# A prefetch hint at the head of the program for the branch over a fallback path

## The chip, the cores and the metric

The kernel runs on one core of one Trainium2 chip. The metric is the device time of one execution in microseconds; three runs of the kernel before took 587.13, 588.6 and 590.96 us, and their median, 588.6 us, is its time. Engines are named as in the profile: PE (TensorE, with PEld for its weight loads), DVE (VectorE), ACT (ScalarE), POOL (GpSimd) and SP (SyncE, which issues the transfers). Each engine has a sequencer that reads its own program, and each program has its own copy of every branch.

## What is computed

A linear attention with a decay per row of the state, and behind it a gated feed-forward layer. B is 4, H 8, S 768, D 48; there are 3072 tokens, 384 features and 1536 hidden features.

```python
state = np.zeros((B, H, D, D))
for t in range(S):
    state = alpha[:, :, t, :, None] * state + np.einsum('bhd,bhe->bhde', k[:, :, t], v[:, :, t])
    y[:, :, t] = np.einsum('bhd,bhde->bhe', q[:, :, t], state)
x = y.transpose(0, 2, 1, 3).reshape(B * S, H * D)
g = x @ w_gate
out = (g / (1 + np.exp(-g)) * (x @ w_val)) @ w_out
```

q, k, v and alpha are 32-bit floats; the three weight matrices arrive as 64-bit floats.

## The kernel before, in words

`tile_kernel` (L1053 to L1065) calls `main_path`, which does all of the work for inputs in the expected ranges, and behind it a branch to `general_path`, a slow second version for any input.

`main_path` cuts the sequence into 16 units of 192 steps, each of three chunks of 64, and computes the recurrence with products on PE (scores, carry, outputs) and scans on DVE. The rows are packed into blocks of 384 tokens. For each of the 8 blocks there are 12 steps over the hidden features: the gate and value products (L692), the silu on ACT (L700), the product with the value on DVE (L704), and the output product (L724). Every factor is split into a high and a low part, and three of the four part products are taken. Weights are cut from 64 bits to single precision by three operations on raw words (L148, L151, L154). The order of everything is written out by hand in the table `ORDER`, one word per step with a letter for the engine (t PE, v DVE, s ACT, g POOL, y SP), and played back at L889 to L896 without a scheduler moving anything.

In parallel the kernel checks that alpha and the weights lie in the ranges for which this method is exact enough. Each check leaves 1 or 0 per partition; a product with ones (L911) sums them, and L912 writes the sum into `flag`: 128 when all partitions are in range. Then come

```python
        ok = nc.values_load(flag[0:1, 0:1], min_val=0, max_val=P)
        with tc.If(ok < P):
            general_path(tc, *args, scratch)
```

at L1063 to L1065. In each engine's program this is a TENSOR_LOAD of the flag into a register (L1063) and a compare-and-branch (L1064). For the inputs timed here the flag is 128, so every engine branches over its part of the general path, which lies directly behind the compare, to a short tail: waits on the semaphores of what this engine, or on SP its transfers, had in flight (also L1064), then, on SP, waits on all of them once more, and twice a barrier of all engines with a clearing of semaphores between (L1091, the line that opens and closes the tile context). SP's last work ahead of the branch is the store of the last three tiles of the result (L741, tiles `ot`), which wait for ACT's copies out of PSUM (L736).

How far the jump goes differs by engine. In rows of the program (one row can stand for several equal instructions), the compare stands at row 1905 of 2457 on PE, 503 of 2281 on DVE, 475 of 681 on ACT, 121 of 138 on POOL and 397 of 615 on SP; the tail is at the end of each.

## Time and profile before

| what | value |
|---|---|
| median of three runs (lowest, highest) | 588.6 us (587.13, 590.96) |
| span of the profiled execution | 586.7 us |
| PE busy | 560.2 us, 95% |
| DVE, ACT, POOL busy | 405.7, 258.9, 128.0 us |
| mean granted TensorE clock | 0.990 |
| last matmul ends | 577.75 us |
| last data packet of a store ends | 581.27 us |

The span runs from the first to the last instruction of the program on any engine; the profile gives no device time of that same execution beside it, so the runs stand above it. Register, branch, semaphore and transfer-issuing instructions are not counted as busy; they show in the view of one source line, under the engine's name with a q (SPq is SP's sequencer, PEldq that of PE). There a row gives the operation, how often it occurs, its shortest, median and longest time in ns, and the start of the first and of the last in us. The view of transfers names the queues that fetch code "instruction".

### The profile page before, as it was taken

The numbers are of one execution on the slowest core, as the hardware profiler recorded it, in microseconds if no ns is written. First come the engines' busy times: TensorE is split into PE (matmuls) and PEld (weight loads), VectorE is DVE, ScalarE is ACT, GpSimd is POOL, SyncE is SP. The second block draws the span as 40 slices with busy tenths as digits, with TensorE's granted clock in tenths as the row PEclk, the third lists the DMA queues.
The fourth block names the chain that finished last, engine by engine and source line by source line (L and its number), as shares of the span: only waits on it lengthen the run. The fifth ranks groups of instructions, "written<-read, shape, count | busy, mean of one in ns | idle before, by whom it ended". The sixth has DMA issues, their size and how long they took to land.

```text
span 586.7 us, 13794 instructions
## 1 busy us (share of the span) xinstructions
PE 560.2 (95%) x5555; PEld 531.0 (91%) x5555; DVE 405.7 (69%) x625; ACT 258.9 (44%) x599; POOL 128.0 (22%) x122
## 2 busy tenths in 40 slices
PE   9899897998999999999999999999999999999993
PEld 4677786888999999999999999999999999999993
DVE  7789999998898999939989859885942321121120
ACT  5587542342331222232326664646565656542121
POOL 6115443452323221222120101400001110001110
PEclk9989999998999999999999999999999999999998
DMA  7799945322235853336485858774553362200001
GB/s 238 243 290 247 332 111 117 82 63 66 76 98 127 199 161 91 85 75 145 105 203 141 192 155 227 198 193 153 175 126 104 92 171 63 62 27 15 1 0 47
DMA packets 95368, 77.67 MB, mean 132 GB/s; under 512 B 32832, under 2 KB 92224, under 8 KB 95296
## 3 DMA queue, kind: packets, MB, share of 16 engines
q1 hardware_dynamic: 95296, 76.71, 49.1%
q8 instruction: 45, 0.74, 0.5%
q14 instruction: 27, 0.22, 0.1%
HBM read 62.52 MB, written 5.90 MB: 117 GB/s over the span
## 4 chain that ended last, share of the span: by engine, by line
PE 77%; DVE 10%; DMA 7%; issue 2%; SPq 2%; POOL 0%; ACT 0%; DVEq 0%
PE v L692 23%; PE ops L724 23%; PE g L692 22%; DMA raw<-in_moe_w_val_dram 3%; PE early_ps L766 2%; PE A L553 2%; DMA raw<-in_moe_w_out_dram 2%; PE s L530 2%; PE y L619 2%; DVE t L151 2%; DVE t L154 1%; DMA raw<-in_moe_w_gate_dram 1%; DVE h L704 1%; DMA L<-in_k_dram 1%; DVE t L148 1%
## 5 line engine op out<-in xcount | busy, mean ns | idle before, releaser
L692 PE MATMUL v<-xT,w 128*128 128x384 f32 x864 | 168.7, 339 | 8.4 <-DVE h L704 8.4
L692 PE MATMUL g<-xT,w 128*128 128x384 f32 x864 | 167.8, 338 | 0.1
L692 PEld LDWEIGHTS v<-xT,w 128*128 128x128 f32 x864 | 151.3, 189 | 11.1 <-DVE h L704 10.3
L724 PE MATMUL ops<-w,hh 128*128 128x384 f32 x576 | 157.7, 337 | 0.0
L692 PEld LDWEIGHTS g<-xT,w 128*128 128x128 f32 x864 | 151.6, 188 | 1.8 <-ACT h L700 0.6
L713 POOL TENSOR_TENSOR hl<-h,hh 128x384 fp32r<-128x384 f32 x54 | 57.6, 1067 | 304.5 <-ACT hh L708 293.5
L704 DVE TENSOR_TENSOR h<-h,v 128x384 f32<-128x384 f32 x96 | 52.9, 551 | 102.5 <-PE v L692 101.1
L708 ACT CAST hh<-h 128x384 fp32r<-128x384 f32 x96 | 49.2, 513 | 140.5 <-DVE h L704 73.8
L724 PEld LDWEIGHTS ops<-w,hh 128*128 128x128 f32 x576 | 105.2, 188 | 0.8
L724 PE MATMUL ops<-w,hl 128*128 128x384 f32 x288 | 97.0, 337 | 1.6 <-DVE hl L713 1.5
L700 ACT ACTIVATE h<-g 128x384 f32<-128x384 f32 x96 | 47.0, 489 | 104.3 <-PE g L692 92.0
L505 DVE STREAM_TRANSPOSE K<-Gs 32x384 f32<-32x384 f32 x96 | 54.7, 570 | 2.4 <-PE A L553 0.6
L724 PEld LDWEIGHTS ops<-w,hl 128*128 128x128 f32 x288 | 54.1, 188 | 2.5 <-DVE hl L713 2.1
L713 DVE TENSOR_TENSOR hl<-h,hh 128x384 fp32r<-128x384 f32 x42 | 26.4, 628 | 26.0 <-ACT hh L708 25.5
L325 POOL TENSOR_TENSOR w<-t,w 128x768 fp32r<-128x768 f32 (+1 forms) x17 | 36.4, 2152 | 30.2 <-ACT w L321 21.3
L448 DVE TENSOR_TENSOR_SCAN AT<-AT,back 128x771 f32<-128x771 f32 x16 | 33.8, 2115 | 0.6
L563 DVE TENSOR_TENSOR X<-s,mask 64x384 f32<-64x384 f32 (+1 forms) x48 | 26.0, 553 | 10.1 <-PE s L530 8.0
L464 POOL TENSOR_TENSOR X<-trq,AT 112x768 f32<-112x768 f32 x9 | 15.8, 1759 | 57.4 <-DMA xT<-X 23.6
L439 DVE TENSOR_TENSOR_SCAN Gs<-AT,inj 128x772 f32<-128x772 f32 x16 | 28.2, 1761 | 0.2
L321 ACT CAST w<-t 128x768 fp32r<-128x768 f32 (+1 forms) x20 | 15.4, 774 | 23.0 <-DVE t L154 22.9
L297 ACT ACTIVATE wc<-wc,wbias 128x384 f32<-128x384 f32 x36 | 23.4, 649 | 1.2
L154 DVE SCALAR_TENSOR_TENSOR t<-raw,t 128x768 uint32<-128x768 uint32 (+1 forms) x20 | 21.4, 1070 | 0.5
(112 smaller groups left out, 591.0 us busy)
## 6 DMA issues: line engine op xcount, KB each, us to landing
xT<-X SPq DMA_DIRECT2D x84, 72.0 KB, 2.2
raw<-in_moe_w_gate_dram SPq DMA_DIRECT2D x12, 384.0 KB, 7.2
raw<-in_moe_w_val_dram SPq DMA_DIRECT2D x12, 384.0 KB, 7.8
V<-in_v_dram SPq DMA_DIRECT2D x96, 48.0 KB, 3.0
raw<-in_moe_w_out_dram SPq DMA_DIRECT2D x12, 384.0 KB, 8.2
wc<-in_moe_w_gate_dram SPq DMA_DIRECT2D x12, 384.0 KB, 5.1
wc<-in_moe_w_val_dram SPq DMA_DIRECT2D x12, 384.0 KB, 3.7
wc<-in_moe_w_out_dram SPq DMA_DIRECT2D x12, 384.0 KB, 4.6
```

Of the source, the lines that this page charges most:

```text
L154: lambda: nc.vector.scalar_tensor_tensor(out=t, in0=lo, scalar=29, in1=t, op0=ALU.logical_shift_right, op1=ALU.bitwise_or),
L325: eng.tensor_tensor(out=lo, in0=src, in1=hi.bitcast(F32), op=ALU.subtract)
L439: nc.vector.tensor_tensor_scan(*(x.rearrange("p g t -> p (g t)")[:, ::-1] for x in (Gs, AT, inj)), 0.0, op0=ALU.mult, op1=ALU.add)
L448: nc.vector.tensor_tensor_scan(Af, Af, back[:, 1 : n + 1], back[:, 0:1], op0=ALU.mult, op1=ALU.add)
L505: nc.vector.transpose(out=bass.AP(k0.tensor, k0.offset, [k0.ap[0], (G * 2 * D, NU), (2 * D, G), (1, 32)]), in_=Kg[j * BO + x : j * BO + x ...
L563: nc.vector.tensor_tensor(out=X[r, z, f * GF : (f + 1) * GF, :].rearrange("r g (c t) -> r g c t", c=NU), in0=sps[f][r].rearrange("r g (c t ...
L692: nc.tensor.matmul(pt, wsp[kind, f][a][:, kt * P : (kt + 1) * P], xT[blk][:, b_, kt, :], start=(n == 0), stop=(n == 3 * KT - 1),)
L700: nc.scalar.activation(h, acc.pop(("g", blk, f)), AF.Silu)
L704: nc.vector.tensor_tensor(out=h, in0=h, in1=acc.pop(("v", blk, f)), op=ALU.mult)
L708: nc.scalar.copy(out=hh, in_=acc["h", blk, f])
L713: eng.tensor_tensor(out=hl, in0=acc.pop(("h", blk, f)), in1=hh.bitcast(F32), op=ALU.subtract)
L724: nc.tensor.matmul(ops[blk][i], h[b_][:, i * P : (i + 1) * P], wsp["o", f][a], start=(first and n == 0), stop=(last and n == 2),)
```

## The change

In front of the playback of `ORDER` one call is added, and the branch is given a label that the call names:

```diff
@@ main_path
             todo[f"wc{i}"] = lambda eng, i=i: range_check(i)
+    tc.mark_branch_hint_location(
+        "right", "LikelyTaken", engines=[e.engine for e in (nc.sync, nc.scalar, nc.vector, nc.tensor, nc.gpsimd)]
+    )
     BANKS = ("A0", "A1", "A2", "ops0", "ops1", "vps", "gps")
@@ tile_kernel
-        with tc.If(ok < P):
+        with tc.If(ok < P, label="right"):
             general_path(tc, *args, scratch)
```

In the built program this is one instruction on each of the five engines, BRANCH_PREFETCH_HINT, which names the branch with that label on the same engine and says that it is likely taken. Although the call stands behind the allocation and clearing of the tiles in the source, the instruction comes out in front of them, second in each program behind the jump that enters the tile context. Nothing else differs in kind, order or waits on any engine; line numbers grow by three (L1064 is L1067 in the changed kernel, L1091 is L1094) and the numbers in the names of tiles by five. SP's program before begins

```order
L1091 UNCONDITIONAL_BRANCH
L423 DMA Le<-in_alpha_dram 128x2x288
L280 DMA raw_132<-in_moe_w_gate_dram 128x3x256
L280 DMA raw_134<-in_moe_w_val_dram 128x3x256
L423 DMA Le<-in_q_dram 128x2x288
```

and with the change

```order
L1094 UNCONDITIONAL_BRANCH
L1094 BRANCH_PREFETCH_HINT
L423 DMA Le<-in_alpha_dram 128x2x288
L280 DMA raw_137<-in_moe_w_gate_dram 128x3x256
L280 DMA raw_139<-in_moe_w_val_dram 128x3x256
L423 DMA Le<-in_q_dram 128x2x288
```

where `Le` and `raw` are tiles for alpha and for raw weights: the hint stands ahead of the first transfer. Around the branch SP's rows with the change are

```order
L1066 TENSOR_LOAD flag
L1066 ISA x2
L741 DMA out_dram<-ot_0_11_6435 128x384
L741 DMA out_dram<-ot_1_11_6437 128x384
L741 DMA out_dram<-ot_2_11_6478 128x384
L741 DMA out_dram<-ot_0_11_6830 128x384
L741 DMA out_dram<-ot_1_11_6832 128x384
L741 DMA out_dram<-ot_2_11_6835 128x384
L1067 COMPARE_AND_BRANCH
L946 COMPARE_AND_BRANCH
L946 UNCONDITIONAL_BRANCH x2
L1094 BRANCH_PREFETCH_HINT
```

The compare at L1067 is the branch that the hint names; the rows behind it belong to the general path, whose two loops had hints of their own for their back edges before the change too. These rows are the same in the kernel before, but for the numbers.

## The prediction

> **What bounds the kernel now.** I read the page first (engines, slices, queues, chain), then the chain in order of time, then everything that stands behind the last matmul, because the change touches one branch and that branch stands there. From the page:

> ```profile
> span 586.7 us, 13794 instructions
> PE 560.2 (95%) x5555; PEld 531.0 (91%) x5555; DVE 405.7 (69%) x625; ACT 258.9 (44%) x599; POOL 128.0 (22%) x122
> PE   9899897998999999999999999999999999999993
> ...
> q8 instruction: 45, 0.74, 0.5%
> q14 instruction: 27, 0.22, 0.1%
> ```

> TensorE (PE) is busy 95% of the span and in every slice but the last. The last two rows are code: the instructions themselves come by DMA, in 45 packets of 16 KB (0.74 MB over 45) on one queue and some 27 of 8 KB on the other. PE has 5555 matmuls and as many weight loads, 11,110 instructions; over 45 packets that is 247 each, so the 16 KB queue feeds PE (about 64 bytes an instruction, 256 to a block), and the 8 KB blocks of the other four engines hold 128. The last slice has PE at 3 tenths. The chain in order of time ends so:

> ```profile
> 571.50 6.26 PE ops L724 x36
> 577.76 0.02 issue
> 577.78 0.48 ACT ot L736
> ```

> and the window view, cut at the last matmul, at the last store's issue and at the end of its data, is

> ```profile
> 577.75:579.60 1.85, 0.00 (x0) 0.00 (x0) 0.00 (x0) 0.48 (x1) 0.00 (x0) 1.00 0.45 153
> 579.60:581.27 1.67, 0.00 (x0) 0.00 (x0) 0.00 (x0) 0.00 (x0) 0.00 (x0) 1.00 0.60 208
> 581.27:586.67 5.40, 0.00 (x0) 0.00 (x0) 0.00 (x0) 0.00 (x0) 0.00 (x0) 0.57 0.02 6
> ```

> (columns: length, then busy time of PE, its loads, DVE, ACT, POOL, the clock, DMA share, GB/s). So 8.9 us lie behind the last matmul, and in the last 5.4 us no engine computes and almost no data moves. What those hold, the view of the branch's line shows; a q behind an engine's name is its sequencer, and the last columns are first and last start:

> ```profile
> L1064 SPq EVENT_SEMAPHORE  x8: 17/17/17, 583.3 to 583.9; - x8
> L1064 POOLq COMPARE_BRANCH  x1: 45/45/45, 567.1 to 567.1; - x1
> L1064 POOLq EVENT_SEMAPHORE  x1: 17/17/17, 567.6 to 567.6; - x1
> L1064 DVEq COMPARE_BRANCH  x1: 72/72/72, 575.8 to 575.8; - x1
> L1064 PEldq COMPARE_BRANCH  x1: 3502/3502/3502, 576.4 to 576.4; - x1
> L1064 ACTq COMPARE_BRANCH  x1: 50/50/50, 578.6 to 578.6; - x1
> L1064 DVEq EVENT_SEMAPHORE  x1: 21/21/21, 578.7 to 578.7; - x1
> L1064 SPq COMPARE_BRANCH  x1: 50/50/50, 579.7 to 579.7; - x1
> L1064 PEldq EVENT_SEMAPHORE  x1: 51/51/51, 580.0 to 580.0; - x1
> L1064 ACTq EVENT_SEMAPHORE  x1: 17/17/17, 581.3 to 581.3; - x1
> ```

> From its branch to its next instruction POOL takes 0.5 us (567.1 to 567.6), DVE 2.9, ACT 2.7, PE 3.6, SP 3.6. POOL has 15 rows of program between its compare and the end, so its jump stays within a block of where it is; the others jump over hundreds. What SP does in that time is nothing: the waits of its queue have

> ```profile
> SPq L1064 <- SPq L1064: 3.7, 1, 3.7
> ```

> a wait on itself. I read these gaps as the fetch of the block that holds the jump's target. [...]

> SP is the last, and behind its eight waits comes a second hole, in the rows of the closing barrier's line, asked for in two windows:

> ```profile
> L1091 SPq EVENT_SEMAPHORE  x2: 28/28/28, 584.0 to 584.1; - x2
> ...
> L1091 SPq EVENT_SEMAPHORE  x8: 17/28/28, 585.5 to 586.6; - x8
> ```

> Two go at 584.0 and 584.1, the next at 585.5: 1.4 us. The code queue in the window 583.5 to 585 has

> ```profile
> q14 instruction: 1, 0.01, 2.1%
> ```

> one 8 KB block. So the jump's target lies near the end of its block, and the next one is asked for only after SP has arrived there. SP's arrival sets the end. ACT, the latest of the other four, stands in the barrier at 581.4:

> ```profile
> L1091 ACTq DRAIN  x2: 8/8/8, 581.4 to 586.2; - x2
> ```

> **The change part by part.** It adds one instruction per engine behind the entry jump, and takes nothing away. I take two terms.

> *The hint's own time.* No hint has run in this trace. The nearest rows are sequencer instructions of the same kind, SP's register moves in the entry (L1080) and the branches above (45 to 72 ns):

> ```profile
> L1080 SPq MOVE  x4: 29/34/42, 0.0 to 0.2; - x4
> ```

> Five engines execute it side by side, so once 0.03 to 0.07 us counts; it is on the path, since the chain starts with them. Above it is bounded by 3.7, if an engine stood still until the block asked for had come; below by nothing, as it removes no work. I take 0.1, by the moves, because a prefetch that stalls its engine would be none.

> *The end.* If the target's block is there when SP branches, SP goes on after 0.5 us as POOL did, at 579.7 + 0.5 = 580.2. It then meets its waits for the stores. The last three stores' rows:

> ```profile
> L741 SPq DMA_DIRECT2D out_dram<-ot x3: 332/332/1095, 577.2 to 579.3; - x3
> ...
> DMA to landing us min/median/max: 2.5/2.6/3.5
> ```

> The last was issued at 579.3 and landed 2.5 later, at 581.8. What was hidden in the fetch till now, the landing, is late next. The eight waits took 0.6 us in a row (583.3 to 583.9); about half of them come behind the landing, 582.1, and the two of the closing line make it 582.3. The following block was ready 2.2 us after SP's arrival in the target's block (583.3 to 585.5); counted from 580.2 that is 582.4, nearly the same instant. From there the end is as before, 586.7 - 585.5 = 1.2 us, so 583.6: a gain of 3.1 us. Bounds: at most 3.3, if the following block is there too (the landing then decides: 582.3 - 0.1 + 1.2 = 583.4); at least nothing, if the target's block isn't there. The added instruction moves every block's end by one instruction, which at 0.08 us each is inside the rounding.

> [...]

> DVE, PE and ACT would save 2.2 to 3.1 us each at their branch, which is worth nothing: they wait in the barrier for SP. The general path is not run, so its loops' own hints play no part.

> Sum: -3.1 + 0.1 = -3.0 us on a span of 586.7, so 583.7. The page has no time of that execution beside its span; the runs have a median of 588.6, 1.9 above the span, and I keep that difference: **585.6 us**.

> **The rivals.**

> *Lost on the way, 588.7 us.* The hint is the first instruction, the branch comes 570 us later; PE refills 45 times in between. If the block is fetched at once, the refills push it out before it is needed, and all that is left is the hint's 0.1. For this: the place, and that all refills seen are in sequence. Against: the hint names a branch by its label, and an instruction that names the branch can be kept until that branch's own block comes in; SP also passes few blocks, its 8 KB packets being a share of 27. [...]

> *The wrong side, 588.7 us.* The condition written, flag below 128, is the one for the general path. If "taken" means that side, the hint asks for the block right behind the branch, which comes in sequence anyway. For this: the text of the change. Against: the general path stands right behind the branch, so the machine's taken jump is the skip, and the four long gaps are paid on that jump.

> *The hint displaces a refill, slower.* While the hint is armed, its block takes the place of the block that comes next in sequence, and an engine waits at the block's end as SP does at 584.1. Place: PE's refills; price: 1.4 us each. One costs less than the end gives (588.7 - 3.1 + 1.4 = 587.0 us); from the third on it decides (589.8), and if all 45 are hit it is 588.7 - 3.1 + 63 = 648.6 us. For it: a prefetcher that has to hold one more block. Against: a refill has 586.7/45 = 13 us of room, and its packets take 0.5% of the DMA engines.

> *A stall in front, 592.3 us.* The hint waits for its fetch (3.7) and the block is lost later: 588.6 + 3.7. Against it: this puts two of the doubtful things together.

> **How the numbers follow.** The forecast has 0.65: the fetch is plainly in the rows and SP stands idle for it, and the doubt is the distance. Lost on the way 0.17, the wrong side 0.07, a refill displaced 0.07 (0.04 of it in the many-refill form), a stall in front 0.04. The forecast's own range is 585.6 with its term's bound (0.2 lower) and the spread of the runs shown (587.1 to 591.0, so -1.5 and +2.4): 583.9 to 588.0. The two cases of no effect, 0.24 together, need 588.7 inside with some spread above it; I leave out the stall and the many refills, and end at 589.3. The runs before lie 0.65% apart, so 1%, 5.9 us, is about what a measurement tells from no change: the forecast, -0.5%, and both cases of no effect lie inside. Faster by over 1% would take the full gain and a median nearly 3 us low, 0.03; slower by over 1% is the many refills and a little of the stall, 0.05; within 1%, 0.92.

> **What would show it.** Right: SP's first wait of the branch's line 0.5 us after its branch instead of 3.6, with the same for DVE, ACT and PE; SP's closing waits reached by 582.4 and no hole over 0.3 us; the code packets for the target's blocks earlier than the branch; the hint's row at the front under 0.1 us. Lost on the way or the wrong side: SP's gap again 3.6 and the code packet behind the branch; for the first, extra code packets in the first microseconds; for the second, none. A displaced refill: holes between PE's matmuls at block ends, which the chain calls issue. I'd be wrong altogether if SP were held by the barrier instead: another engine arriving after SP.

## The result, and the profile after

| | before | with the hint |
|---|---|---|
| median (lowest, highest) of 10 runs | 588.98 us (585.01, 591.78) | 585.7 us (582.64, 587.46) |
| span of the profiled execution | 586.7 us | 584.0 us |
| last matmul ends | 577.75 | 577.88 |
| SP's branch starts | 579.7 | 580.1 |
| from SP's branch to the end | 7.0 | 3.9 |

The ratio of the times is 0.9945, with a 95% interval of 0.992 to 0.997: 0.55% faster, 3.2 us. In the two profiles all of it lies behind SP's branch. The rows of the branch's line in the changed kernel (L1067):

```profile
L1067 SPq EVENT_SEMAPHORE  x8: 17/17/17, 582.0 to 582.6; - x8
L1067 POOLq COMPARE_BRANCH  x1: 59/59/59, 567.2 to 567.2; - x1
L1067 POOLq EVENT_SEMAPHORE  x1: 17/17/17, 567.7 to 567.7; - x1
L1067 DVEq COMPARE_BRANCH  x1: 84/84/84, 576.0 to 576.0; - x1
L1067 PEldq COMPARE_BRANCH  x1: 398/398/398, 576.6 to 576.6; - x1
L1067 DVEq EVENT_SEMAPHORE  x1: 21/21/21, 576.6 to 576.6; - x1
...
L1067 ACTq COMPARE_BRANCH  x1: 68/68/68, 578.7 to 578.7; - x1
L1067 ACTq EVENT_SEMAPHORE  x1: 17/17/17, 579.2 to 579.2; - x1
L1067 SPq COMPARE_BRANCH  x1: 70/70/70, 580.1 to 580.1; - x1
```

DVE goes on 0.6 us after its branch (2.9 before), ACT 0.5 (2.7), and PE's branch takes 398 ns instead of 3502. SP goes on after 2.0 us (1.97 before the starts are rounded to 580.1 and 582.0), 1.7 less than before, yet about four times as long as DVE and ACT. The line that closes the tile context (L1094):

```profile
L1094 SPq EVENT_SEMAPHORE  x10: 17/28/28, 582.6 to 583.9; - x10
...
L1094 POOLq BRANCH_PREFETCH_HINT  x1: 51/51/51, 0.8 to 0.8; - x1
L1094 SPq BRANCH_PREFETCH_HINT  x1: 65/65/65, 0.8 to 0.8; - x1
L1094 ACTq BRANCH_PREFETCH_HINT  x1: 45/45/45, 0.8 to 0.8; - x1
L1094 DVEq BRANCH_PREFETCH_HINT  x1: 51/51/51, 0.9 to 0.9; - x1
L1094 PEldq BRANCH_PREFETCH_HINT  x1: 50/50/50, 0.9 to 0.9; - x1
```

SP's ten closing waits take 1.3 us (582.6 to 583.9) where they took 2.6 (584.0 to 586.6): the hole of 1.4 us behind the second of them is gone. The hints cost 45 to 65 ns each. The windows, cut as before at the last matmul, in the last store and at the end of its data:

```profile
577.88:580.00 2.12, 0.00 (x1) 0.00 (x0) 0.00 (x0) 0.48 (x1) 0.00 (x0) 1.00 0.40 139
580.00:581.65 1.65, 0.00 (x0) 0.00 (x0) 0.00 (x0) 0.00 (x0) 0.00 (x0) 1.00 0.52 189
581.65:583.97 2.32, 0.00 (x0) 0.00 (x0) 0.00 (x0) 0.00 (x0) 0.00 (x0) 0.79 0.01 4
```

The idle stretch behind the data has gone from 5.4 to 2.3 us; the stretch ahead of it has grown a little. So the 3.1 us from branch to end are two pieces, 1.7 of SP's gap and 1.4 of the hole; 0.4 is given back ahead of the branch. There the last matmul ends 0.1 us later than before, and the longest of SP's last three stores takes 1325 ns to issue instead of 1095:

```profile
L741 SPq DMA_DIRECT2D out_dram<-ot x3: 332/333/1325, 577.4 to 579.7; - x3
...
DMA to landing us min/median/max: 2.3/2.8/3.6
```

### The profile page after: what moved, and what is told of

It reads as the page before. It is cut to its first block, busy times and chain, and to the rows that moved or that the text cites. A ratio compares the mean times of both kernels' runs of the same rounds, so it can differ in the third digit from the quotient of the medians.

```text
span 584.0 us, 13799 instructions
## 1 busy us (share of the span) xinstructions
PE 561.9 (96%) x5555; PEld 532.6 (91%) x5555; DVE 406.0 (70%) x625; ACT 258.8 (44%) x599; POOL 126.9 (22%) x122
## 4 chain that ended last, share of the span: by engine, by line
PE 77%; DVE 11%; DMA 6%; issue 2%; SPq 2%; POOL 0%; ACT 0%; DVEq 0%
PE ops L724 23%; PE v L692 23%; PE g L692 22%; DMA raw<-in_moe_w_gate_dram 2%; DVE t L151 2%; PE early_ps L766 2%; PE A L553 2%; PE s L530 2%; PE y L619 2%; DMA raw<-in_moe_w_out_dram 2%; DMA raw<-in_moe_w_val_dram 1%; DVE t L154 1%; DMA L<-in_k_dram 1%; DVE h L704 1%; DVE t L148 1%
## 5 line engine op out<-in xcount | busy, mean ns | idle before, releaser
L724 PE MATMUL ops<-w,hh 128*128 128x384 f32 x576 | 157.7, 337 | 0.0
L724 PEld LDWEIGHTS ops<-w,hh 128*128 128x128 f32 x576 | 105.2, 188 | 0.8
L724 PE MATMUL ops<-w,hl 128*128 128x384 f32 x288 | 97.0, 337 | 1.5 <-DVE hl L713 1.5
L724 PEld LDWEIGHTS ops<-w,hl 128*128 128x128 f32 x288 | 54.1, 188 | 2.4 <-DVE hl L713 2.1
L553 PE MATMUL A<-V,K 64*48 64x48 f32 (+1 forms) x720 | 21.5, 207 | 0.5 <-DVE X L563 0.3
```

The costliest lines, as they stand in the source:

```text
L553: nc.tensor.matmul(to[j * BO : j * BO + D, g - gs.start, :], Ks[r, x, g, KC[j]], Vd[r, x, g, VC[j]], start=(x == 0 or not whole), stop=(x ...
L724: nc.tensor.matmul(ops[blk][i], h[b_][:, i * P : (i + 1) * P], wsp["o", f][a], start=(first and n == 0), stop=(last and n == 2),)
```

## The experiments

Theory A, formed on these rows: the hint makes an engine fetch the jump's target on entering the code block that holds the branch, instead of the block next in sequence, and SP enters that block only half a microsecond ahead of its branch, which is why it still waits; only SP's jump counts. The rivals stand in each expectation. The profiled executions differ by a few microseconds in the body ahead, so the traces are compared from SP's branch to the end, and the times by their ratio to the kernel before on the same chip. Gaps are differences of printed starts, so they can be off by 0.1 us.

| run | SP's gap behind its branch, us | hole in the closing waits | branch to end | ratio to before (95%) |
|---|---|---|---|---|
| before | 3.6 | 1.4 | 7.0 | 1 |
| the change | 2.0 | none | 3.9 | 0.9945 (0.992 to 0.997) |
| hint on SP alone | 1.9 | none | 3.9 | 0.9949 (0.9926 to 0.9971) |
| hint on all but SP | 3.4 | none | 5.4 | 0.9976 (0.9947 to 1.0006) |
| one drain, no hint | 3.3 | 1.6 | 6.9 | 1.0005 (0.9974 to 1.0036) |
| twelve drains, no hint | 2.9 | none | 4.8 | 0.9943 (0.992 to 0.9966) |
| hint, eleven drains | 0.5 | none | 3.6 | 0.9922 (0.9898 to 0.9947) |
| hint, one drain | 0.7 | none | 4.0 | 0.9958 (0.9939 to 0.9977) |
| hint, eleven drains, drain on PE | 0.5 | none | 3.3 | 0.9929 (0.99 to 0.9959) |
| drain on PE, no hint | 3.4 | 1.5 | 6.8 | 0.999 (0.9967 to 1.0013) |
| no branch | - | - | - | 0.9926 (0.9893 to 0.9959) |

The intervals of the runs with the hint on SP, of twelve drains and of no branch all lie below 1 and overlap, so the times don't rank these runs. What is said below of single pieces rests on the traces, one execution each.

Two things in the traces bear on theory A. First, the start of the block that holds the branch shows as a pause of about 0.35 us in front of one of SP's instructions: its last store in the kernel before, the instruction ahead of that store with the change or with one drain, the middle store with the hint and one drain. In the kernel before, SP has such a pause, of 0.34 to 0.36 us, at 160.71, 244.91, 325.68, 398.50 and 579.27 us, each time 128 of its rows after the last; so the prediction's 128 to a block holds for SP, and PE's 16 KB packets start 255 of PE's rows apart in the mean of 42 intervals. By this the branch's block starts 0.4, 0.5 and 1.7 us ahead of the branch. Second, in the seven traces with such a pause an 8 KB code packet starts 0.7 to 0.8 us behind the block's start. Their queue is not SP's alone (in the kernel before, packets on it start at 576.86, 1.0 us behind DVE's branch, and at 579.30, 0.7 behind ACT's); I take as SP's the packets that no branch or arrival of another engine explains.

**The hint on SP alone.**

```diff
-    tc.mark_branch_hint_location(
-        "right", "LikelyTaken", engines=[e.engine for e in (nc.sync, nc.scalar, nc.vector, nc.tensor, nc.gpsimd)]
-    )
+    tc.mark_branch_hint_location("right", "LikelyTaken", engines=[e.engine for e in (nc.sync,)])
```

> The hint on SP alone. Theory A (the armed hint makes SP, on entering the block that holds the branch, fetch the jump's target in place of the block next in sequence; only SP's jump sets the end): all of the gain is here. SP goes on 2.0 us after its branch, no hole in the closing waits, span 2.7 us under the 586.7 of before, time about 585.8; the gaps of DVE, PE and ACT are back at 2.9, 3.6 and 2.7 us. Rival B (an engine other than SP also counts): part of the gain is missing, 587 or more. Rival C (the added instruction only moved SP's code to other places in its blocks) gives the same as A here.

Measured: 585.38 us. The rows of its branch's line:

```profile
L1065 SPq EVENT_SEMAPHORE  x8: 17/17/17, 582.5 to 583.1; - x8
...
L1065 PEldq COMPARE_BRANCH  x1: 3842/3842/3842, 576.9 to 576.9; - x1
...
L1065 SPq COMPARE_BRANCH  x1: 70/70/70, 580.6 to 580.6; - x1
```

The whole gain is there with PE (3842 ns), DVE and ACT paying for their jumps as before. Rival B falls: what the other four save is worth nothing.

**The hint on all but SP.**

```diff
-    tc.mark_branch_hint_location(
-        "right", "LikelyTaken", engines=[e.engine for e in (nc.sync, nc.scalar, nc.vector, nc.tensor, nc.gpsimd)]
-    )
+    tc.mark_branch_hint_location("right", "LikelyTaken", engines=[e.engine for e in (nc.scalar, nc.vector, nc.tensor, nc.gpsimd)])
```

> The hint on the other four engines. Theory A and rival C: no gain, time as before (588.6 to 589), SP's gap 3.7 and the hole of 1.4 us in its closing waits as before, although DVE, PE and ACT go on 0.5 to 0.6 us after their branches. Rival B: part of the gain, 1 us or more.

Measured: 586.27 us; the interval of its ratio holds 1, so a gain shows in the trace alone. SP's rows in the branch's line and in the closing one (here L1092):

```profile
L1065 SPq EVENT_SEMAPHORE  x8: 17/17/17, 581.4 to 582.0; - x8
...
L1065 SPq COMPARE_BRANCH  x1: 50/50/50, 578.0 to 578.0; - x1
```
```profile
L1092 SPq EVENT_SEMAPHORE  x10: 17/28/28, 582.0 to 583.3; - x10
```

I expected no gain, and theory A missed half of what happened. The gap is nearly as long as before, 3.4 us, but the hole is gone (ten waits in 1.3 us), although SP's instructions are those of the kernel before. The built program shows one difference on SP: the label that the skip jumps to carries a mark on all engines, be the hint on all five, on these four or on SP alone, and none without a hint. I conclude that the marked target is put at the start of a code block, so that SP needs no second one. The trace agrees: a next block starts to come at 582.2, 0.8 us behind SP's arrival, and SP runs to its end without waiting for it, where in the kernel before the next block starts 0.6 us behind SP's arrival and SP stands for it. That the mark is what moves the target is argued from these rows and the next run, not seen by itself. So the hole goes with hints on the other four engines alone, and only the 1.7 us of the gap need the hint on SP.

**One drain on SP instead of the hint.**

```diff
         for word in ORDER.split():
+            if word == "y:Lc0":
+                for _ in range(1):
+                    nc.sync.drain(fusable=False)
```

> No hint; one drain more in SP's program at a place where SP has time, so that everything behind it stands one instruction later, as with the hint. Rival C: the gain is as with the hint, SP's gap 2.0, no hole, span about 584. Theory A: SP's gap stays over 3 us (its fetch of the block next in sequence starts one instruction earlier, so 3.2 to 3.7), the gain is under 0.6 us; the hole of 1.4 us may stay or go, and tells whether it hangs on the hint or on the place of the target in its block: if it goes, 2 us of gain in all at most.

Measured: 588.25 us, no gain; gap 3.3 us. The closing line, asked for in two windows:

```profile
L1094 SPq EVENT_SEMAPHORE  x1: 28/28/28, 586.8 to 586.8; - x1
...
L1094 SPq EVENT_SEMAPHORE  x9: 17/28/28, 588.4 to 589.6; - x9
```

Before, two closing waits ran and then came the hole; with one instruction more ahead, one runs and then it comes. The hole is tied to a fixed place in the program's blocks, as a block's end is, and rival C falls: moving the code by one does not give the gain.

**Twelve drains on SP, no hint** (the same edit with 12).

> No hint; twelve drains more in SP's program at the same place. Theory A: the branch now stands 13 instructions behind its block's start, so SP entered this block long before and the fetch of the block next in sequence is over when it branches; only the target's fetch is left, a gap of 2.7 to 2.9 us as on ACT and DVE, 0.9 less than before; and the target falls behind the next block's start, so there is no hole: 2.2 us of gain, time about 586.6. A theory by which SP's long gap is the traffic of the stores on the same transfer engines: the gap stays 3.7, only the hole goes, 587.4.

Measured: 585.76 us, 0.8 under the 586.6 expected, and by the times as much as with the hint; by the trace the end is 0.9 us longer than with the hint (4.8 against 3.9) and 2.2 shorter than before, as expected. SP's rows:

```profile
L1067 SPq EVENT_SEMAPHORE  x8: 17/17/17, 582.5 to 583.0; - x8
...
L1067 SPq COMPARE_BRANCH  x1: 50/50/50, 579.6 to 579.6; - x1
```

The gap is 2.9 us with the stores still in flight, so their traffic isn't the reason for the 3.6; and it agrees with 0.8 us spent, in the kernel before, on the block next in sequence, which SP had asked for just ahead of its branch and never used. The code packets bear this out: in the kernel before one starts at 579.98, 0.7 us behind SP's entry into the branch's block, and the next, the target's, at 581.55, 1.9 behind the branch; here only one of SP's lies between its branch and its arrival, 1.3 behind the branch, at 580.89. The other 1.4 of this run's gain is the hole; that it went because the target now lies behind the next block's start is argued.

**The hint and eleven drains on SP** (the hint as in the change; the loop as above with 11).

> The hint as in the change and eleven drains more in SP's program, so that the branch stands 13 instructions behind the start of its code block, which SP then enters some 70 us ahead. Theory A (the armed hint makes SP fetch the target on entering the branch's block, and the lead was only half a microsecond): SP goes on 0.5 us after its branch; it is then held at the fourth of its eight waits by the last store's landing, and the end lies 1.7 us behind that landing. From branch to end 3.6 us, 0.3 less than with the change alone (3.9), time 585.0 to 585.5. A rival by which SP's 2.0 us with the hint is a fixed price of the jump or the stores' traffic: the gap stays 2.0, 3.9 from branch to end.

Measured: 584.27 us. SP's rows:

```profile
L1070 SPq EVENT_SEMAPHORE  x8: 17/17/17, 578.8 to 580.5; - x8
...
L1070 SPq COMPARE_BRANCH  x1: 70/70/70, 578.3 to 578.3; - x1
```

With the block entered early the gap is 0.5 us, and the eight waits, 0.6 us in a row before, now take 1.7: they wait for the stores. From branch to end it is 3.6 us, as expected; the time came out 0.7 us under the expected range of 585.0 to 585.5. The 2.0 us of the change were neither a fixed price nor the landing. The view of transfers from 499 to 500 us shows what SP did on entering the block:

```profile
q14 instruction: 1, 0.01, 1.9%
```

**The hint and one drain on SP** (the loop with 1).

> The hint as in the change and one drain more, so that SP enters the branch's block one instruction earlier, with the second of the last three stores, about 2.2 us ahead of the branch. Theory A: the target's fetch starts 0.7 us after that entry, and takes 0.4 us and 1.4 more until SP can go on, so it is ready 0 to 0.4 us after the branch: SP's gap 0.5 to 0.7 us. The rival (fixed price or traffic): 2.0 as with the change, since one instruction is 0.07 us.

Measured: 586.64 us, gap 0.7 us:

```profile
L1070 SPq EVENT_SEMAPHORE  x8: 17/17/17, 582.8 to 584.7; - x8
...
L1070 SPq COMPARE_BRANCH  x1: 70/70/70, 582.1 to 582.1; - x1
```

One instruction of 0.07 us takes 1.3 us off the gap. That fits a fetch which starts on entering the branch's block: the block now begins one instruction earlier in SP's program, with the store that takes over a microsecond to issue. The target's packet starts at 581.04, 0.7 us behind the entry and 1.0 ahead of the branch. With the change it stands 0.8 us behind the entry, at 580.41, and so 0.3 behind the branch (view of transfers from 580.1 to 581.5):

```profile
q14 instruction: 1, 0.01, 1.4%
```

From branch to end it is 4.0, no better than the change, since the last store landed later, 2.3 us behind the branch instead of 1.9; the intervals of the times overlap.

**No branch.** The `If` and the general path are left out, so inputs out of range are not treated.

```diff
-        with tc.If(ok < P):
-            general_path(tc, *args, scratch)
```

> The branch and the general path are left out, so an input out of range would not be treated; there is no jump and no target to fetch. This is the floor of what any hint can do: the landing of the last store decides. Theory A: no gap over 0.6 us behind SP's last store but the landing's, from the last store's issue to the end 2.3 us to the landing and 1.4 to 1.7 behind it, 3.7 to 4.1 (with the change 4.3, before 7.4); time 584.7 to 585.5. If something else than code fetch fills the end (the barrier, the stores), it stays as long as with the change.

Measured: 584.19 us, 0.5 under the expected range; span 580.2. From the last store's issue to the end it is 3.1 us, less than the 3.7 to 4.1 expected, and 3.6 from the last matmul. This row shows why:

```profile
L741 SPq DMA_DIRECT2D out_dram<-ot x3: 332/332/335, 576.1 to 577.2; - x3
...
DMA to landing us min/median/max: 1.9/1.9/1.9
```

All three stores take 0.33 us to issue and land after 1.9, where in every kernel with the branch so far the middle one takes 1.1 to 1.5 and they land after 2.2 to 4.1. Something of the branch reaches ahead of it. In those traces PE branches at this time, and a 16 KB code block of PE starts to come 1.0 to 1.2 us later; without the branch no such block comes in the last 12 us.

**A drain on PE.** The runs with eleven drains and the hint, and the kernel before, each with

```diff
                 todo.pop(name)(engines[e], *(BANKS[int(x)] for x in "".join(banks)))
+            if word == "t:o95":
+                nc.tensor.drain(fusable=False)
```

> As the run with the hint and eleven drains on SP, with one drain on PE behind its last matmul, so that PE's sequencer reads the flag and branches only when the last product is done (about 1.5 us later), and the 16 KB code block that PE asks for on arriving at the target comes later too. Theory D (SP's second-to-last store is held up by PE's code block: in the six runs with that block at this time it takes 1.1 to 1.4 us and the next instruction follows about 0.4 us behind the block's end; without a branch it takes 0.33): the store takes 0.33 us, the last store is issued 0.6 us behind the last matmul instead of 1.7, the landing and the end come about 1.1 earlier, 4.4 to 4.8 us from the last matmul to the end instead of 5.7; time 583.0 to 583.6. Rival E (the store is held by something of SP's own): 5.7 as before, 584.3.

> The kernel before with the one drain on PE alone. Theory D: SP's last store is issued 0.6 us behind the last matmul instead of 1.5, so the end comes about 0.9 earlier, 8.0 instead of 8.9 us from the last matmul to the end; PE now misses its target later, goes on 3.6 us behind a branch at 578.4, that is at 582, and still waits for SP. Time 587.5 to 587.8. Rival E: no change, 8.9, 588.5.

Measured: 584.06 and 587.97 us, 0.5 over the range expected for the first and 0.2 over that for the second. PE's branch now stands 1.0 us behind the last matmul's end instead of 1.3 ahead of it, 2.3 us later and not 1.5. The stores of the first, and of the second:

```profile
L741 SPq DMA_DIRECT2D out_dram<-ot x3: 332/333/333, 577.7 to 578.7; - x3
...
DMA to landing us min/median/max: 1.9/1.9/1.9
```
```profile
L741 SPq DMA_DIRECT2D out_dram<-ot x3: 332/332/333, 578.1 to 579.4; - x3
...
DMA to landing us min/median/max: 1.9/1.9/3.1
```

In the first the view knows the landing of one store alone; SP's waits for the other two end 1.9 and 2.0 us behind their issue. The last matmul ends at 578.2 and the span at 582.4: 4.2 us, less than the 4.4 to 4.8 expected, against 5.7 with the hint and eleven drains alone, 6.1 with the change and 8.9 before. In the kernel before with the drain on PE it is 8.0, as expected. Rival E falls: what held the store hangs on when PE branches. In the times neither of these can be told from the same kernel without the drain; by its trace the first has the shortest end of all that still treat every input.

The traces show what of PE it is. The 16 KB block in the window from 577 to 578.6 us before, and in that from 575.9 to 577.5 with the hint and eleven drains:

```profile
q8 instruction: 1, 0.02, 4.0%
```
```profile
q8 instruction: 1, 0.02, 5.3%
```

Shares are of 16 engines over 1.6 us, so the block took 1.0 and 1.4 us; the middle store took 1095 and 1538 ns. In all eight traces with a long middle store its issue ends 0.38 us (0.380 to 0.386) behind the end of this block, which took 1.03 to 1.39 us. Counted from PE's branch the same end varies by 0.4 us. PE's arrival at its target can't be what holds the store: without a hint on PE it comes behind the end of the store's issue (580.0 against 578.9 before). With the drain on PE the block starts only at 580.9 and 581.1, behind the issue of all three stores, and in the second run it overlaps the landing that takes 3.1 us.

## Why the prediction was right

Time, sign and size were right, 585.7 us where 585.6 was forecast. Of the two terms the hint's own time held; the end held only in its sum, by luck.

- *What bounds the end.* Right. SP's jump sets it, and the fetch of code behind it; with the hint on SP alone the end is as short as with the change.
- *The hint's own time*, 0.1 us. Right: 45 to 65 ns.
- *SP goes on after 0.5 us.* Wrong: 2.0. I took the block to be there well ahead, and the fetch begins only on entering the branch's block, half a microsecond earlier. One of my signs of being right, the target's packet ahead of the branch, was not there for SP: it came 0.3 us behind. With the branch deeper in its block the 0.5 was measured. (By the row numbers above, 17 rows stand behind POOL's compare, not 15; nothing hangs on it.)
- *The following block is ready 2.2 us after SP's arrival, and the hole shrinks to it.* Wrong: the hole went altogether, and with hints on the other four engines alone too. My shift of one instruction was costed at nothing, and rightly so, but I hadn't thought of the target being placed otherwise.
- *The sum*, 3.1 us behind the branch. Right by two errors that cancelled: 1.5 us too little wait behind the branch, and 1.4 too much from there to the third closing wait, 2.2 us by the prediction (580.2 to 582.4) where 0.75 was measured. The 1.2 us behind that held. Measured it is 7.0 to 3.9.
- *The landing is late next.* It was level with the fetch: the last store, issued at 579.7, landed 2.3 us later at 582.0, when SP went on. It is late next once the gap is gone: with eleven drains the end is 3.6 us behind the branch, by the prediction's own bound, the landing, 3.7.
- *The difference of time and span* carried over: the median lay 1.9 us above the span before (588.6 and 586.7, the times on which the forecast rests), and 1.7 after (585.7 and 584.0).
- *Rivals.* Lost on the way and the wrong side fall by SP's gap and by the run with eleven drains. No refill was displaced: PE's 16 KB code packets went from 45 to 44. Nothing stalled in front.

Without a hint I read SP's packet on entering the branch's block (in the kernel before at 579.98, 0.7 us behind the entry) as the next block in sequence, which SP never used. With the hint at the very front (65 ns at 0.8 us on SP, in the change) the target's block came on entry in place of the next one (499.16 in the run with eleven drains, with no other packet of SP's before it arrived at the target), some 500 us after the hint.

## What to carry to other kernels

Look at what lies behind the last matmul with the view of one source line: sequencer instructions count as busy nowhere, and over three of the nine microseconds there were waits for code (8.9 us before, of which a gap of 3.6 and a hole of 1.4 on SP; the change took off 3.1). Here a hint on a jump was worth its fetch only on the engine that arrives last, and in full only where that engine entered the branch's block well ahead (1.7 us were nearly enough, 0.5 were not). A dozen cheap instructions in a place with time took 2.2 us off the end, the hint 3.1, both together 3.4 by the traces; the times don't tell the three apart. When a predicted sum comes out right, check the parts: here both parts of the end were off.

## What the runs showed of the hardware that I had not expected

- On SP the hint acted when SP came into the block of the branch (the target's packet started 0.8 us behind that with the change, 0.7 with the hint and one drain), and the target then came in place of the next block. With a lead of two instructions the gap was 2.0 us, of three, with a slow store among them, 0.7, of thirteen 0.5. Where SP waited for the target's packet, it went on 1.2 to 1.5 us behind the packet's end.
- SP's jump without a hint cost the fetch in sequence too, where that had just begun: a gap of 3.6 us, and of 2.9 with the block entered early.
- PE's code block delayed SP's stores. With PE branching ahead of its last matmuls' end the middle store took 1.1 to 1.5 us to issue, until 0.38 us behind the block's end, and the stores landed after 2.2 to 4.1 us; with PE branching 2.3 us later it took 0.33 and they landed after 1.9 (but for the last store of the run without a hint, after 3.1). Why a 16 KB block should hold up the issue of a store stays open.
